# Reading three of four batches in large loads: a gated linear attention and a feed-forward layer on one core

## The chip, the cores and the metric

The kernel runs on one core of a Trainium2 chip. The metric is the device time of one execution in microseconds. Two runs of the kernel before took 193.17 and 194.55 us, median 193.86. A profiled execution gives the trace that this document reads; its span, from the first to the last instruction of the program, is 192.0 us.

The core has a matrix engine (PE, with its weight loads shown apart as PEld), a vector engine (DVE), an activation engine (ACT), GpSimd (POOL), and a sync engine (SP), which issues every DMA transfer of this kernel on one queue. The queue is served by 16 DMA engines.

## What is computed

Gated linear attention over 4 batches, 8 heads, 768 steps and 48 dimensions, followed by a feed-forward layer over the 3072 tokens:

```python
for t in range(S):
    state = alpha[:, :, t, :, None] * state + np.einsum('bhd,bhe->bhde', k[:, :, t], v[:, :, t])
    y[:, :, t] = np.einsum('bhd,bhde->bhe', q[:, :, t], state)
...
x = y.transpose(0, 2, 1, 3).reshape(B * S, H * D)      # 3072 x 384
h = x @ w_in                                           # 384 -> 2048
r = np.maximum(h, 0.0)
out = (s * (r * r) + b) @ w_out                        # 2048 -> 384
```

Inputs and outputs are 32-bit floats. q, k, v and alpha have 4.72 MB each.

## The kernel before

The sequence is cut into 24 blocks of 128 steps, six to a batch. A block n goes through these steps, named by the functions that issue them:

- Four loads (`load`, L192 to L197), one for each of alpha, q, k, v: 128 partitions (the steps) by 8 heads by 48 floats, 196,608 bytes, in pieces of 192 bytes, since consecutive steps of a head go to different partitions. Each tensor has five buffers (`NIN`), so the load of block n + 5 may be issued when block n has been read.
- `st_ln` (ACT) takes the logarithm of alpha; `st_cum` (PE) sums it along the steps; `st_exp_b` and `st_exp_i` (ACT) give the gates b and 1/b; `st_qb` and `st_kb` (DVE) multiply q and k by them; `st_vcast` (POOL) casts v.
- q and k are transposed: blocks 0 to 7 (`NPE`) by PE into PSUM with a copy on DVE (`st_T`, `st_Tcopy`), later ones by a DMA transpose on the SP queue (`st_Tdma`, L355).
- `st_A` (PE) makes the products of q and k, `st_mask` (DVE) masks them, `st_KV` (PE), `st_t1` (DVE) and `st_snew` (POOL) carry the state on, `st_y` (PE) makes the block's output and `st_yevac` (ACT) moves it to SBUF as the input of the feed-forward layer. From block 9 (`NAY`) y(n-1) is issued together with A(n).
- The feed-forward layer works on groups of one or two blocks (`GROUPS`): `mm1` units (PE) into two PSUM banks, `relu` (ACT), `square` (DVE) into a ring of 12 blocks (`RING`, `gt_sb`), then four `mm2` quads (PE) to a block into two banks `o_ps`, `oevac` (DVE) into three buffers `o_sb`, and `ostore`, a store on the SP queue.

The weights come in eight loads of 768 KB through four staging buffers `wst`, are cast by ACT and, for w_out, summed by DVE (`colsum_part`, `colsum_add`).

The order of the instructions on each engine is written out ahead by a planner, `Schedule` (L43 to L130): every step is an `op` with an engine, a planned duration, a priority, what it reads and what it writes. The planner plays these through with its own durations (a block load 1.02 us on SP, a DMA transpose 1.95) and emits the instructions in the order that comes out. On the chip each engine then runs its list strictly in this order, and waits at each instruction for the semaphores that it needs. So a wait on PE or on SP holds everything behind it. The DMAs take turns on eight semaphores; each waits for the landing of the one eight before it.

`LOADS` (L41) gives the order of the first loads, between which the weights stand.

The functions that the change touches, and what calls them:

Of the kernel before, what the change touches and what calls it, by code (L numbers as in the profile page):

```python
# [18 lines left out]
UNIT = 0.756  # L19
LEAD = {1: 98.3, 2: 224.9, 4: 115.8}  # L20

NPE = 8

NAY = 9

RING = 12

NST = 4

TB = 1.02  # L30
TW = 2.15
FILL_GAP = 0.45

P_BM, P_CS, P_BMM = -5, -380.7, 485.1
P = dict(
# [98 lines left out]
def kernel(  # L134
# [20 lines left out]
    d_model = moe_w_in.shape[0]  # L155
    d_ff = moe_w_in.shape[1]
    NJ = d_ff // 128
    NIN = 5

    sb = ctx.enter_context(tc.tile_pool(name="sb", bufs=1))  # L160
    ps = ctx.enter_context(tc.tile_pool(name="ps", bufs=1, space=bass.MemoryType.PSUM))
# [13 lines left out]
    def many(name, n, shape, dtype, zero=None):  # L175
        tiles = []
        for i in range(n):
            t = sb.tile(shape, dtype, name=f"{name}{i}")
            if zero is not None:
                zero.memset(t, 0.0)  # L180
            tiles.append(t)
        return tiles


    a_in = many("a_in", NIN, [128, H, D], FP32)
    q_in = many("q_in", NIN, [128, H, D], FP32)
    k_in = many("k_in", NIN, [128, H, D], FP32)
    v_in = many("v_in", NIN, [128, H, D], FP32)
    s_col = sb.tile([128, 1], FP32, name="s_col")
    b_col = sb.tile([128, 1], FP32, name="b_col")  # L190

    def load(n, src, dst):  # L192
        b, c = n // NCH, n % NCH
        nc.sync.dma_start(  # L194
            out=dst[n % NIN],
            in_=src[b, :, c * C : (c + 1) * C, :].rearrange("h s d -> s h d"),
        )  # L197

    for src, dst in ((alpha, a_in), (q, q_in), (k, k_in), (v, v_in)):
# [28 lines left out]
    w_in_bf = sb.tile([128, 3, d_ff], BF16, name="w_in_bf")  # L228
    w_out_bf = sb.tile([128, NJ, d_model], BF16, name="w_out_bf")
    QW = 4 * d_model  # L230
    wst = many("wst", NST, [128, QW], FP32)
    colsum = sb.tile([128, 2 * d_model], FP32, name="colsum")
    colpart = sb.tile([128, 2 * d_model], FP32, name="colpart")
    bones = sb.tile([128, 128], FP32, name="bones")
# [63 lines left out]

    def st_ln(n):
        nc.scalar.activation(  # L300
            out=la_sb[n % 2][:, :, 0:D], in_=a_in[n % NIN], func=AF.Ln
        )

    def st_cum(n):
# [21 lines left out]
    def st_vcast(n):  # L326
        nc.gpsimd.tensor_copy(  # L327
            out=vp_sb[n % 4].rearrange("a p (x d) -> a p x d", d=D)[:, :, 0:3:2, :],
            in_=v_in[n % NIN].rearrange("a (p e) d -> a p e d", e=2),
        )  # L330

    def st_qb(n):
        nc.vector.tensor_tensor(  # L333
            out=qk_sb[n % 3][:, 0, :, 0:D], in0=q_in[n % NIN], in1=b_sb[n % 2], op=ALU.mult
        )

    def st_kb(n):
        nc.vector.tensor_tensor(  # L338
            out=qk_sb[n % 3][:, 1, :, 0:D],
            in0=k_in[n % NIN],  # L340
            in1=binv_sb[n % 2],
            op=ALU.mult,
        )
# [213 lines left out]
    op("ACT", 2.2, -9000, lambda: None)  # L557
    SRC = {"a": (alpha, a_in), "q": (q, q_in), "k": (k, k_in), "v": (v, v_in)}
    loads = list(LOADS)
    for n in range(1, NBLK):  # L560
        loads += [f"{x}{n}" for x in "aqkv" if f"{x}{n}" not in LOADS]

    def load_op(x, n):
        op("SP", TB, loads.index(f"{x}{n}") - 1000, load, n, *SRC[x], w=[(x, n % NIN)], lat=2.0)

    stage = 0
    for x in range(4):
        op("SP", 1.4 if x == 0 else 0.85, -2000 + x, lambda: None, w=[("aqkv"[x], 0)], lat=2.0)
    for rank, item in enumerate(loads):
        t, i = rank - 1000, int(item[1:])  # L570
        if item[0] in "aqkv":
            if i < NIN:
                load_op(item[0], i)
# [28 lines left out]
    def add_block(n):  # L602
        i2, i3, ii = n % 2, n % 3, n % NIN
        t = want(n)
        if n >= NIN:
            for x in "aqkv":
                load_op(x, n)
        op("ACT", 0.45, t + P["ln"], st_ln, n, r=[("a", ii)], w=[("la", i2)])
        op("PE", 0.27, t + P["cum"], st_cum, n, r=[("la", i2)], w=["ct"], lat=0.16)
        op("ACT", 0.41, t + P["eb"], st_exp_b, n, r=["ct"], w=[("b", i2)])  # L610
        op("ACT", 0.49, t + P["ei"], st_exp_i, n, r=["ct"], w=[("bi", i2), ("bl", i2)])
        op("POOL", 0.5, t + P["vc"], st_vcast, n, r=[("v", ii)], w=[("vp", n % 4)], lock=True)
        op("DVE", 0.48, t + P["qb"], st_qb, n, r=[("q", ii), ("b", i2)], w=[("qb", i3)], lock=True)
        op("DVE", 0.48, t + P["kb"], st_kb, n, r=[("k", ii), ("bi", i2)], w=[("kb", i3)], lock=True)
# [12 lines left out]
        late = n + 1 < NBLK and n + 1 >= NAY  # L627
        if n >= NAY:
            r1, w1 = ys.pop(n - 1)
            op("PE", 0.935, want(n - 1) + P["Ay"], st_Ay, n, r=rA + r1, w=wA + w1, lat=0.16)  # L630
            yevac_op(n - 1)
        else:
            op("PE", 0.43, t + P["A"], st_A, n, r=rA, w=wA, lat=0.16)
        op("DVE", 1.14, t + P["mk"], st_mask, n, r=["a"], w=[("am", i2)])
        rr = [("am", i2), ("qkT", i3), ("vp", n % 4)] + ([] if first(n) else [("S", (n - 1) % 3)])
        if late:
            ys[n] = (rr, ["py"])
        else:
            op("PE", 0.6, t + P["y"], st_y, n, r=rr, w=["py"], lat=0.16)
            yevac_op(n)  # L640
# [29 lines left out]
                op("SP", 0.55, -2000, ostore, x, r=[("os", (x // 4) % 3)])  # L670

    for n in range(NBLK):
        add_block(n)

        if n and n >= NAY and blk_group[n - 1][0] != blk_group[n][0]:
            add_group(blk_group[n - 1][0])
        if (n + 1 < NAY or n + 1 == NBLK) and n + 1 == first_blk[blk_group[n][0]] + GROUPS[blk_group[n][0]]:
            add_group(blk_group[n][0])

    def fill(idle, at):
        for _ in range(int((idle - FILL_GAP) / (0.22 if at < 9.0 else 0.12))):
# [35 lines left out]
```

## Time and profile before

| what | value |
|---|---|
| median of two runs | 193.86 us |
| span of the profiled execution | 192.0 us (1.8 less than the median) |
| PE busy | 175.3 us, 91% |
| DVE, ACT, POOL busy | 135.9, 109.5, 33.3 us |
| DMA queue of SP | 124,192 packets, 34.09 MB, 82.6% of 16 engines' span |
| read from and written to HBM | 25.17 MB, 4.72 MB |
| last matmul ends | 188.5 us |
| mean granted clock of PE | 0.991 |

How to read the profile: the page gives each engine's busy time and, in 40 equal slices of 4.8 us, the busy share in tenths. The DMA line is the mean busy share of the 16 DMA engines. The table by stretches gives the same for chosen stretches of the span. The chain of waits follows back from the last instruction what released what. In lists of instructions a line starts with the time since the span's start and the duration; "x6" are instructions run together. Matmuls are pipelined, and their ends are modelled, so the distance between starts tells more than a busy time.

### The profile page before, as it was taken

What the parts mean: (1) busy time and instruction counts of PE and PEld (TensorE: products, weight loads), DVE (VectorE), ACT (ScalarE), POOL (GpSimd) and SP (SyncE); (2) the same over time, 40 slices, a digit from 0 to 9 for tenths busy, and PEclk for the clock granted to TensorE, in tenths of its full rate; (3) what the DMA queues carried; (4) which work ended last, traced back from release to release, by engine and by line L of the source; (5) the groups of instructions that cost most, each with busy time, mean ns of one, the idle gap of its engine ahead of it and who ended that gap; (6) DMA issues with size and microseconds to landing.
All of it is one profiled execution on the core that took longest, in us unless ns stands there. A gap on an engine that the chain in (4) does not pass through costs nothing.

```text
span 192.0 us, 5369 instructions
## 1 busy us (share of the span) xinstructions
PE 175.3 (91%) x2153; PEld 126.7 (66%) x2153; DVE 135.9 (71%) x256; ACT 109.5 (57%) x225; POOL 33.3 (17%) x60
## 2 busy tenths in 40 slices
PE   1877688879999999999999999999999999999992
PEld 0555467657677767777777766776766876777761
DVE  4643299989799898877689868587777786554421
ACT  3254789984357847767475754763663763654300
POOL 8402022103120431201122313011131131000000
PEclk9996999999999999999999999999999999999999
DMA  6989979999999999999999998897998895011112
GB/s 122 203 219 317 312 161 245 353 223 205 196 232 193 219 140 213 197 214 188 196 160 209 145 236 188 171 207 169 208 197 195 164 180 144 3 43 41 40 45 82
DMA packets 124218, 34.44 MB, mean 179 GB/s; under 512 B 117536, under 2 KB 122656, under 8 KB 124192
## 3 DMA queue, kind: packets, MB, share of 16 engines
q1 hardware_dynamic: 124192, 34.09, 82.6%
q8 instruction: 17, 0.28, 0.6%
q14 instruction: 9, 0.07, 0.1%
HBM read 25.17 MB, written 4.72 MB: 156 GB/s over the span
## 4 chain that ended last, share of the span: by engine, by line
PE 66%; DMA 14%; DVE 8%; SPq 7%; ACT 2%; issue 1%
PE o_ps L515 29%; PE h_ps L490 25%; PE py_ps L444 5%; DMA wst<-in_moe_w_in_dram 4%; DMA q_in<-in_q_dram 4%; SPq L194 4%; DMA wst<-in_moe_w_out_dram 3%; PE a_ps L406 3%; SPq L240 3%; DMA qkT<-qk 3%; DVE am L415 2%; PE py_ps L364 2%; PE ct_ps L306 1%; DVE gt L506 1%; ACT r L499 1%
## 5 line engine op out<-in xcount | busy, mean ns | idle before, releaser
L490 PE MATMUL h_ps<-xd,w_in_bf 128*128 128x256 bf16 (+1 forms) x624 | 74.8, 264 | 0.8 <-ACT r L499 0.5
L499 ACT ACTIVATE r<-h_ps 128x512 bf16<-128x512 f32 x96 | 56.5, 601 | 32.3 <-PE h_ps L490 22.8
L515 PE MATMUL o_ps<-w_out_bf,gt 128*128 128x384 bf16 x384 | 72.8, 326 | 2.0 <-ACT w_out_bf L261 2.0
L490 PEld LDWEIGHTS <-w_in_bf 128*128 128x128 bf16 x624 | 54.7, 98 | 10.8 <-issue 1.2
L506 DVE TENSOR_TENSOR gt<-r 128x512 bf16<-128x512 bf16 x96 | 43.5, 465 | 21.7 <-ACT r L499 21.1
L515 PEld LDWEIGHTS <-gt 128*128 128x128 bf16 x384 | 36.0, 98 | 21.2 <-issue 2.3
L415 DVE TENSOR_TENSOR am<-a_ps,mask 128x1024 bf16<-128x1024 f32 x24 | 29.3, 1220 | 1.6 <-PE a_ps L406 1.4
L327 POOL CAST vp<-v_in 128x384 bf16<-128x384 f32 x24 | 13.3, 553 | 95.0 <-DMA v_in<-in_v_dram 84.7
L526 DVE SCALAR_TENSOR_TENSOR o_sb<-o_ps,s_col,bias_w 128x384 f32<-128x384 f32 x24 | 14.8, 616 | 10.0 <-PE o_ps L515 9.6
L300 ACT ACTIVATE la<-a_in 128x384 bf16<-128x384 f32 x24 | 12.5, 521 | 14.1 <-DMA a_in<-in_alpha_dram 13.9
L400 POOL TENSOR_TENSOR s_st<-t,blast 128x384 bf16<-128x384 bf16 x16 | 14.5, 909 | 30.8 <-DVE t L389 23.0
L468 ACT ACTIVATE xd<-py_ps 128x384 bf16<-128x384 f32 x24 | 11.8, 491 | 13.0 <-PE py_ps L444 12.8
L338 DVE TENSOR_TENSOR qk<-k_in,binv 128x384 bf16<-128x384 f32 x24 | 13.4, 558 | 6.7 <-ACT binv L323 5.5
L333 DVE TENSOR_TENSOR qk<-q_in,b_s 128x384 bf16<-128x384 f32 x24 | 13.5, 564 | 5.2 <-ACT b_s L320 4.1
L320 ACT ACTIVATE b_s<-ct_ps 128x384 f32<-128x384 f32 x24 | 11.7, 488 | 6.8 <-PE ct_ps L311 6.7
L389 DVE TENSOR_TENSOR t<-py_ps,s_st 64x192 bf16<-64x192 f32 x32 | 11.3, 353 | 3.9 <-PE py_ps L364 3.2
L306 PE MATMUL ct_ps<-la,U_bf 128*128 128x384 bf16 x24 | 8.0, 334 | 6.3 <-ACT la L300 6.3
L323 ACT ACTIVATE binv<-ct_ps 128x384 f32<-128x384 f32 x24 | 11.8, 490 | 0.0
L311 PEld LDWEIGHTS <-la 128*128 128x128 bf16 x96 | 6.0, 97 | 7.7 <-issue 5.6
L406 PE MATMUL a_ps<-qkT 64*128 64x128 bf16 x192 | 9.8, 222 | 1.0 <-DVE qkT L373 0.7
L406 PEld LDWEIGHTS <-qkT 64*128 64x128 bf16 x192 | 5.5, 96 | 7.3 <-issue 4.3
L444 PE MATMUL py_ps<-am,vp 128*32 128x128 bf16 x384 | 9.8, 224 | 0.5 <-DVE am L415 0.5
(42 smaller groups left out, 108.1 us busy)
## 6 DMA issues: line engine op xcount, KB each, us to landing
a_in<-in_alpha_dram SPq DMA_DIRECT2D x24, 192.0 KB, 3.9
q_in<-in_q_dram SPq DMA_DIRECT2D x24, 192.0 KB, 3.9
k_in<-in_k_dram SPq DMA_DIRECT2D x24, 192.0 KB, 3.9
v_in<-in_v_dram SPq DMA_DIRECT2D x24, 192.0 KB, 3.7
out_dram<-o_sb SPq DMA_DIRECT2D x24, 192.0 KB, 2.6
wst<-in_moe_w_in_dram SPq DMA_DIRECT2D x4, 768.0 KB, 8.4
wst<-in_moe_w_out_dram SPq DMA_DIRECT2D x4, 768.0 KB, 7.0
qkT<-qk SPq DMA_TRANSPOSE x16, 3.7
```

Source lines behind the costliest of these rows:

```text
L327: nc.gpsimd.tensor_copy(out=vp_sb[n % 4].rearrange("a p (x d) -> a p x d", d=D)[:, :, 0:3:2, :], in_=v_in[n % NIN].rearrange("a (p e) d -> ...
L333: nc.vector.tensor_tensor(out=qk_sb[n % 3][:, 0, :, 0:D], in0=q_in[n % NIN], in1=b_sb[n % 2], op=ALU.mult)
L338: nc.vector.tensor_tensor(out=qk_sb[n % 3][:, 1, :, 0:D], in0=k_in[n % NIN], in1=binv_sb[n % 2], op=ALU.mult,)
L400: nc.gpsimd.tensor_tensor(out=s_sb[n % 3], in0=t1_sb[n % 2], in1=bl, op=ALU.mult)
L406: nc.tensor.matmul(out=a_ps[:, e, p, :], lhsT=qkT[64 * e : 64 * e + 64, 1, p, :], rhs=qkT[64 * e : 64 * e + 64, 0, p, :], start=True, stop ...
L415: nc.vector.tensor_tensor(out=am_sb[n % 2].rearrange("a e p t -> a (e p) t"), in0=a_ps.rearrange("a e p t -> a (e p) t"), in1=mask.unsquee ...
L444: nc.tensor.matmul(out=y_ps[32 * (x % 4) : 32 * (x % 4) + 32, x // 4, :], lhsT=(st[:, p, c0 : c0 + 32] if e is None else vp[:, p, c0 + 48 ...
L490: nc.tensor.matmul(out=hp[:, i * n : (i + 1) * n], lhsT=w_in_bf[:, kk, 128 * j : 128 * (j + 1)], rhs=xd_sb[g % 3][:, kk, 0:n], start=(kk = ...
L499: nc.scalar.activation(out=r_sb[w % 2], in_=h_ps[w % 2], func=AF.Relu)
L506: nc.vector.tensor_tensor(out=gt_sb[:, js[0] : js[0] + len(js), c0 : c0 + n], in0=r, in1=r, op=ALU.mult)
L515: nc.tensor.matmul(out=op[:, 0:d_model], lhsT=gt_sb[:, j, c0 : c0 + C], rhs=w_out_bf[:, j, :], start=(j == 0), stop=(j == NJ - 1),)
L526: nc.vector.scalar_tensor_tensor(out=ots, in0=o_ps[(x // 4) % 2][:, 0:d_model], scalar=s_col, in1=bias_w, op0=ALU.mult, op1=ALU.add,)
```

## The change

The four inputs move into two sets of buffers, each of which holds a whole batch of all four tensors. The blocks of batch 0 are loaded one by one as before. Batches 1, 2 and 3 are loaded tensor by tensor: one load of 1,179,648 bytes brings a tensor's six blocks (`load_batch`). The loads of batch 1 stand behind the 24 block loads; those of batch 2 are ordered behind the k products of blocks 8 to 11, those of batch 3 behind those of blocks 14 to 17 (`BATCH_AT`; this is an order in the planner's list, not a wait on the chip). The four staging buffers of the weights become a part of the second set, so batch 1's alpha, q and k wait for the casts and sums that read them. PE transposes blocks 0 to 6 instead of 0 to 7, and the ring has 10 blocks instead of 12. At the end five more loads of q (`probe`) are issued into the first set, in pieces of 2, 3, 4 and 6 rows and of one row; what they bring is not used. They overlap in the buffer, so each waits for the one before.

```diff
-NPE = 8
+NPE = 7
-RING = 12
+RING = 10
+TBATCH = 3.2
+BATCH_AT = {1: 1, 2: 8, 3: 14}
...
-    a_in = many("a_in", NIN, [128, H, D], FP32)
-    q_in = many("q_in", NIN, [128, H, D], FP32)
-    k_in = many("k_in", NIN, [128, H, D], FP32)
-    v_in = many("v_in", NIN, [128, H, D], FP32)
+    in_sb = many("in_set", 2, [128, 4, H, NCH, D], FP32)
+    a_in, q_in, k_in, v_in = range(4)
+
+    def block_in(x, n):
+        return in_sb[n // NCH % 2][:, x, :, n % NCH, :]
...
+    def load_batch(b, src, dst):
+        nc.sync.dma_start(
+            out=in_sb[b % 2][:, dst].rearrange("a h c d -> a (h c) d"),
+            in_=src[b].rearrange("h (c p) d -> p (h c) d", p=C),
+        )
...
-    wst = many("wst", NST, [128, QW], FP32)
+    stage_sb = in_sb[1].rearrange("a x h c d -> a (x h c d)")
+    wst = [stage_sb[:, QW * i : QW * (i + 1)] for i in range(NST)]
...
-    for n in range(1, NBLK):
+    for n in range(1, NCH):
         loads += [f"{x}{n}" for x in "aqkv" if f"{x}{n}" not in LOADS]
+
+    NIN = 2 * NCH
...
+    def batch_op(x, b):
+        held = [("wst", i) for i in range(NST)] if b == 1 else []
+        op("SP", TBATCH, 4 * b + "aqkv".index(x) - 900, load_batch, b, *SRC[x],
+           r=[("begun", n) for n in [BATCH_AT[b] + "aqkv".index(x)] if b > 1],
+           w=[(x, (NCH * b + c) % NIN) for c in range(NCH)] + held, lat=2.0)
+
+    flat = in_sb[0].rearrange("a x h c d -> a (x h c d)")
+
+    def probe(m):
+        if m:
+            nc.sync.dma_start(
+                out=flat[:, 0 : H * m * D].rearrange("a (h r) -> a h r", h=H),
+                in_=q[0, :, 0 : m * C, :].rearrange("h (p r) d -> p h (r d)", p=C),
+            )
+        else:
+            nc.sync.dma_start(
+                out=flat[:, 0 : 64 * H * NCH].rearrange("a (j d) -> a j d", d=64)[:, :, 0:D],
+                in_=q[0].rearrange("h (c p) d -> p (h c) d", p=C),
+            )
...
-        if n >= NIN:
-            for x in "aqkv":
-                load_op(x, n)
...
     for n in range(NBLK):
+        for b in BATCH_AT:
+            if 0 <= n - 1 - BATCH_AT[b] < 4:
+                batch_op("aqkv"[n - 1 - BATCH_AT[b]], b)
         add_block(n)
...
+    for m in (2, 3, 4, 6, 0):
+        op("SP", 2.0, 5000, probe, m, r=[("qkT", (NBLK - 1) % 3)], w=["probe"])
```

More of the change, by code (lines that the diff above doesn't have):

```diff
@@ L157 @@
     NJ = d_ff // 128
-    NIN = 5
     sb = ctx.enter_context(tc.tile_pool(name="sb", bufs=1))
@@ L194, in load @@
         nc.sync.dma_start(
-            out=dst[n % NIN],
+            out=block_in(dst, n),
             in_=src[b, :, c * C : (c + 1) * C, :].rearrange("h s d -> s h d"),
+        )
[3 more added lines that the diff above has]
+            in_=src[b].rearrange("h (c p) d -> p (h c) d", p=C),
         )
@@ L300, in st_ln @@
         nc.scalar.activation(
-            out=la_sb[n % 2][:, :, 0:D], in_=a_in[n % NIN], func=AF.Ln
+            out=la_sb[n % 2][:, :, 0:D], in_=block_in(a_in, n), func=AF.Ln
         )
@@ L328, in st_vcast @@
             out=vp_sb[n % 4].rearrange("a p (x d) -> a p x d", d=D)[:, :, 0:3:2, :],
-            in_=v_in[n % NIN].rearrange("a (p e) d -> a p e d", e=2),
+            in_=block_in(v_in, n).rearrange("a (p e) d -> a p e d", e=2),
         )
@@ L333, in st_qb @@
         nc.vector.tensor_tensor(
-            out=qk_sb[n % 3][:, 0, :, 0:D], in0=q_in[n % NIN], in1=b_sb[n % 2], op=ALU.mult
+            out=qk_sb[n % 3][:, 0, :, 0:D], in0=block_in(q_in, n), in1=b_sb[n % 2], op=ALU.mult
         )
@@ L339, in st_kb @@
             out=qk_sb[n % 3][:, 1, :, 0:D],
-            in0=k_in[n % NIN],
+            in0=block_in(k_in, n),
             in1=binv_sb[n % 2],
@@ L571 @@
         if item[0] in "aqkv":
-            if i < NIN:
-                load_op(item[0], i)
+            load_op(item[0], i)
             continue
@@ L613, in add_block @@
         op("DVE", 0.48, t + P["qb"], st_qb, n, r=[("q", ii), ("b", i2)], w=[("qb", i3)], lock=True)
-        op("DVE", 0.48, t + P["kb"], st_kb, n, r=[("k", ii), ("bi", i2)], w=[("kb", i3)], lock=True)
+        op("DVE", 0.48, t + P["kb"], st_kb, n, r=[("k", ii), ("bi", i2)], w=[("kb", i3), ("begun", n)], lock=True)
         if n < NPE:
```

## The prediction, made before the changed kernel ran

> **What bounds the kernel now.** I read the page first: busy shares and the 40 slices.
>
> ```profile
> PE 175.3 (91%) x2153; PEld 126.7 (66%) x2153; DVE 135.9 (71%) x256; ACT 109.5 (57%) x225; POOL 33.3 (17%) x60
> ...
> PE   1877688879999999999999999999999999999992
> ...
> DMA  6989979999999999999999998897998895011112
> ```
>
> PE has no gap after slice 10 (48 us), and the DMA engines hardly any from 20 us to 160: two resources are full at once, and the order in which the queue serves them decides. The table by stretches says the same in numbers:
>
> ```profile
> 20.00:48.00 28.00, 23.58 (x336) 18.17 (x336) 23.50 (x41) 23.15 (x41) 4.64 (x6) 1.00 0.98 248
> 48.00:66.00 18.00, 18.00 (x245) 12.52 (x243) 16.01 (x31) 11.15 (x28) 2.99 (x7) 1.00 1.00 209
> 66.00:100.00 34.00, 34.00 (x434) 25.14 (x431) 27.54 (x55) 21.56 (x48) 6.95 (x10) 1.00 0.99 190
> ```
>
> (Stretch, its length, busy us of PE, PEld, DVE, ACT and POOL, granted clock, DMA share, GB/s.) Up to 48 us PE starves on first loads and weights; then it is never idle.
>
> What a load costs the DMA engines shows in the DMA view of 44 to 48 us, where nothing but block loads moves:
>
> ```profile
> DMA packets 4219, 0.80 MB, mean 200 GB/s; under 512 B 4219, under 2 KB 4219, under 8 KB 4219
> ...
> q1 hardware_dynamic: 4219, 0.80, 102.6%
> ```
>
> 0.80 MB in 4219 packets is 190 B each, one 48-float row; 16 engines x 4 us x 1.026 / 4219 = 15.6 ns per piece per engine. Several loads were queued, so this is no latency but the engines' rate for such pieces. The same view of 33.6 to 38.4 us, where half of the packets are weight rows of 1.5 KB, has
>
> ```profile
> DMA packets 2046, 1.69 MB, mean 353 GB/s; under 512 B 1072, under 2 KB 2046, under 8 KB 2046
> ```
>
> so the rate goes with the size of the piece.
>
> That one queue serves in order shows at the transposes (L355). Issue to landing is min/median/max
>
> ```profile
> DMA to landing us min/median/max: 3.0/3.7/4.9
> ```
>
> and the 4.9 is the piece of the chain of waits at 106 us, where two loads had been issued just ahead (104.15 and 104.59):
>
> ```profile
> 105.88 0.55 DVE qk L338
> 106.43 0.03 DVE gt L506
> 106.46 4.92 DMA qkT<-qk
> 111.38 0.05 issue
> 111.42 0.40 PE a_ps L406 x8
> ```
>
> PE takes up A(15) 0.04 us after the landing: there is little room behind a transpose.
>
> **The change, part by part.** Times are those of the profiled execution: span 192.0, 1.8 below the median of the runs (193.86); I add that 1.8 to every span.
>
> *Up to A(5), nothing.* The first 34 DMAs stand in the same order and carry the same bytes in the same 192 B pieces. Their SBUF side becomes strided for blocks 0 to 5; bounds nothing to one more packet cost per piece; I take nothing, since the pieces were counted as 192 B when the SBUF side was one 1,536 B run. A(5) stands at 51.7 us in the PE timeline. What PE has left from there I count in the changed program's order, by starts in the timeline: 80 mm1 units x 0.655, 87 mm2 quads x 0.65, 19 y (16 x 0.51, 3 x 0.34), 19 A x 0.33, 18 cum x 0.27, 18 KV x 0.17, one T 0.45: 132.5 us. Before it is 133.0 (T(7) more), and that took 136.8, to 188.5. So if no wait is added the time is 193.86 - 0.45 = **193.4**. There is nothing else to win: the change takes no other work off PE.
>
> *Batch loads.* 72 block loads become 12 of 6144 pieces. At 200 GB/s one takes **5.9 us**. Lower bound 3.4 (the weights' 353 GB/s), upper 6.2 (190 GB/s, 66 to 100 us). I take 5.9: the pieces stay 192 B, and 200 GB/s is the row of such pieces alone. The planner laid out the new order with 3.2 (TBATCH), so that order has no room for the difference. SP issues 54 rows fewer; it was not the bound, so this is worth nothing, and if issuing one batch takes SP some us, the queue is busy with that batch meanwhile.
>
> The Trainium skill, "DMA: Bandwidth & Descriptors", section "Rules for kernel authors", says the opposite: use 1 MiB or more per DMA, and merge small transfers into one; its table of measurements gives 341 GB/s at 1 MB. By that page a batch would take an estimated 3.5 us. No run here shows that size with such pieces; the rate is rival 1.
>
> *Batch 1 (blocks 6 to 11).* Before, cum(6) needed one load of 0.98 us; now it needs a whole batch. v5 is issued at 43.51 and lands 4.2 later, 47.7. The first batch (alpha) lands 5.9 later, 53.6; Ln 0.52; cum(6) at 54.2 instead of 52.0: stall 2.2. Batch q lands at 60.1 (a store of 0.6 between). Batch k stands on SP behind the stores of blocks 1 and 2, of which the second waits for o_sb at about 57.7; q still fills the queue then, so k lands at 60.1 + 1.2 + 5.9 = 67.2, v at 73.1. PE reaches T(6) at 54.2 + 10.5 of work = 64.7; kb(6) is done at 67.8: stall 3.1. Then A(6), cum(7), cum(8), KV(6) at 73.9 (v and 0.55 of cast); after two more quads all matmul work of blocks 0 to 5 is used up. y(6), its evacuation, KV(7), A(7), mask 1.22, y(7), the transpose of block 8 behind the last evacuation on DVE: A(8) at about 79.5. Without stalls PE would be there at 51.7 + 19.5 = 71.2. Lost: **8.3**. (The casts and column sums of the staging area end at 42.5 and 42.3, before the batch loads over it are issued at 44.7 to 58: that wait is nothing.)
>
> *Batch 2 between the transposes.* On SP: T8, a, T9, q, T10, k, T11, v, T12. Each T waits for a whole batch in the queue ahead of it. T itself takes 1.2 to 1.75 of the queue (it lands 0.8 to 2.7 after the load ahead of it); I take 1.5. So A(8) to A(12) takes 4 x (5.9 + 1.5) = 29.6, against 18.4 of PE work standing there: 11.2 lost, and 1.2 more since KV(12) needs v of the same batch. Lost: **12.4**, A(12) at 110.3.
>
> *Batch 3.* a stands before T14, q before T16, k before T17, v between T18 and T19. The same sum against PE's work: 0.6 at A(14), 1.8 at A(16), 1.9 at A(17), 2.7 at KV(18). Lost: **7.0**.
>
> *NPE 7.* T(7) leaves PE (0.45, counted) and DVE (copy 0.69, not the bound), and adds 1.5 to the queue, inside batch 1's loss. *RING 10:* mm1 is at most some four blocks ahead of mm2 in the order; nothing.
>
> *Probes.* 4.13 MB, each waiting on SP for the landing of the one before: 12 to 21 us of data and five latencies of 2 (the fastest load lands 2.9 after its issue, 1 of it data): 22 to 31. Behind them on SP stand the stores of blocks 14 and 15, behind these DVE's evacuations (three o_sb), then PE (two o_ps). They begin after the store of block 13, with some 50 us of PE work to come, and the DMA engines are near idle there (slices 34 on): nothing, and 1 for 1 past that cover.
>
> Sum: 193.4 + 8.3 + 12.4 + 7.0 = **221**.
>
> A bound that needs no stall table: from 46.3 (v5's data in) the queue must carry 12 x 5.9 + 17 x 1.5 + 13 stores x 0.6 = 104 before T(23) lands at 151.7, and in the new order 42.4 us of PE work (24.8 before) follow A(23). With 1.2 of PE slack, 3.5 from last matmul to end and the 1.8: 201.
>
> **Clock.** Idle PE can cost more than the idle time:
>
> ```profile
> 12.30:15.70 3.40, 1.46 (x21) 1.08 (x22) 1.92 (x2) 1.48 (x1) 0.51 (x1) 1.00 0.65 176
> 15.70:19.10 3.40, 3.38 (x43) 2.27 (x40) 0.71 (x2) 1.49 (x1) 0.83 (x1) 0.52 1.01 320
> ```
>
> After 3.4 us with PE 43% busy, the next 3.4 ran at 0.52. In the stretch A(8) to A(12) PE is busy about 60%, so single windows can fall that low; each costs at most 1.7, part of it inside a wait. I put nothing in the sum and up to 7 in the range. The Trainium skill, "TensorE: Matmul & The Clock Gate", section "Why this matters for your kernels", warns of idle gaps over about 3 us; the trace agrees, and lost the clock even with shorter gaps (longest 1.5). By that page only the 3 us waits count, two or three of them, an estimated 3 to 5 us.
>
> **Rivals.**
> 1. *A batch moves at the weights' rate* (353 GB/s, 3.4 us). Batch 1 then still empties PE around A(7) (mask, transpose latency): 2.9; A(8) to A(12) needs 4 x 4.9 = 19.6 against 18.4, unevenly (A(10) has 3.2 of PE work against 4.9): 3 in all. 193.4 + 6 = **200**. For: one long contiguous run per partition in SBUF. Against: the packets above. This is also where the page's rule leads.
> 2. *Not slower.* The engines pay per SBUF run (9,216 B a partition in a batch) and not per DRAM row. From 4 x (t + 1.5) = 18.4 a batch of t = 3.1 us or less (380 GB/s) hides every transpose; what stays is the chain around A(7), 1.8: **195**. Against: block loads had 1,536 B runs there and were still paid as 192 B.
> 3. *The queue is as forecast, but the rest reacts worse:* the half clock, or probes that hold the last stores: **232** and more.
>
> **Chances.** Forecast 0.84, rival 1 0.08, rival 2 0.05, rival 3 0.03. The range goes from rival 1 to the forecast plus clock and rounding of a dozen stalls, 200 to 232. About 2% is what a measurement here tells from no change: faster 0.01, same 0.05, slower 0.94.
>
> **What would show it.** Right: batch loads landing 6 us apart; transposes L355 with a median near 8 us; PE idle before A (L406) and cum(6) between 52 and 145, 25 to 30 us in all; last 40 us PE full. Wrong: GB/s above 300 while batches move, transposes near 4 us, or PE idle mostly in the last 40 us (probes).

## The result and the profile after

| | before | after |
|---|---|---|
| median of two runs (us) | 193.86 (193.17 to 194.55) | 224.45 (223.84 to 225.06) |
| span of the profiled execution (us) | 192.0 | 222.4 |
| PE busy (us), mean granted clock | 175.3, 0.991 | 182.5, 0.962 |
| packets of SP's queue | 124,192 | 74,704 |

The changed kernel takes 1.161 times as long (95% interval 1.143 to 1.179). That is 3.5 us above the forecast of 221 and inside its range of 200 to 232. Some runs of the experiments below are over 1.5% slower than the fastest of the same kernel; medians and ratios leave them out, and only the traces of e2_split and e11_reverse are of such runs.

The page of the changed kernel: busy shares, then the lines of the 40 slices (5.56 us each) for PE, the granted clock and the DMA engines, and the packet count.

```profile
PE 182.5 (82%) x2145; PEld 129.8 (58%) x2145; DVE 135.3 (61%) x255; ACT 110.9 (50%) x225; POOL 34.2 (15%) x60
...
PE   2875797797968774983997938969999999999993
...
PEclk9999999999999978598899996999999999999999
DMA  6999899998798486989979899783346573951011
...
DMA packets 74728, 38.81 MB, mean 174 GB/s; under 512 B 45008, under 2 KB 73168, under 8 KB 74704
```

Before, PE had no gap from slice 10 on. Now it has gaps up to slice 27 (150 us), which is where batch 3 has landed, and is full behind that. The DMA engines, hardly ever idle before, have dips between 60 and 150 us. The table by stretches (stretch, its length, busy us of PE, PEld, DVE, ACT, POOL, granted clock, DMA share, GB/s) gives this time first for the kernel before, then for the changed one:

```profile
60.00:150.00 90.00, 89.26 (x1129) 64.80 (x1127) 70.83 (x137) 54.36 (x123) 16.68 (x24) 1.00 1.00 191
60.00:150.00 90.00, 68.63 (x832) 47.08 (x831) 55.84 (x105) 43.74 (x101) 14.67 (x22) 0.91 0.92 186
```

So the queue is a little worse used: 0.92 instead of 1.00 of the time, 186 GB/s instead of 191. But the inputs as a whole do not come later. The last load of all, v of batch 3, lands at 149.4 us; before, v of block 23 landed at 159.2. What comes later is what is needed first: v of block 18, the first of batch 3, landed at 126.9 before and lands at 149.4 now.

The same table gives the stages of batches 2 and 3 and the rest:

```profile
80.00:113.00 33.00, 25.44 (x270) 17.08 (x266) 18.46 (x36) 15.43 (x36) 4.58 (x7) 0.79 0.96 188
113.00:152.00 39.00, 31.24 (x434) 22.41 (x434) 26.04 (x50) 20.14 (x47) 7.12 (x10) 0.96 0.93 185
152.00:182.00 30.00, 30.00 (x437) 21.89 (x435) 23.61 (x44) 16.66 (x36) 6.14 (x7) 1.00 0.51 124
```

In 80 to 113 us PE issued 270 matmuls; the kernel before issued 416 there, and its clock stayed at 1.00.

SP's own list from the first load of batch 2 on (start, and the time that SP spent on the issue):

```profile
78.21 0.71 SPq L203 DMA_DIRECT2D in_set<-in_alpha_dram  x1
79.53 6.64 SPq L365 DMA_TRANSPOSE qkT<-qk  x1
86.63 0.69 SPq L203 DMA_DIRECT2D in_set<-in_q_dram  x1
88.92 4.55 SPq L365 DMA_TRANSPOSE qkT<-qk  x1
93.94 0.69 SPq L203 DMA_DIRECT2D in_set<-in_k_dram  x1
```

A transpose is issued 0.9 to 2.3 us after a batch, and SP is held in that issue for 4.6 to 7.0 us (before, the issue took 1.2 to 2.2). The packet records show what ends it: the first one is let go at 86.2, as the transpose's own packets of 256 B begin at 86.0, where those of the batch end. Only then can SP issue the next batch, whose data start at 88.0, after a pause. The fine stretches show the pause: the DMA share falls from 0.97 to 0.68 between two batches. They show the clock too, 0.57 and 0.51 around the wait.

```profile
80.00:84.00 4.00, 4.00 (x30) 2.84 (x25) 3.14 (x6) 1.59 (x3) 1.10 (x2) 0.57 0.97 230
84.00:87.00 3.00, 0.87 (x11) 0.71 (x9) 0.89 (x3) 0.13 (x1) 0.82 (x1) 1.00 0.68 137
87.00:94.00 7.00, 6.08 (x62) 4.05 (x62) 2.34 (x3) 3.65 (x10) 0.00 (x0) 0.51 0.92 196
```

For all 17 DMA transposes together, issue to landing is min/median/max

```profile
DMA to landing us min/median/max: 3.0/4.8/8.8
```

The eight behind a batch take 6.4 to 8.8 each (seven of them 8.3 or more), the others 3.1 to 4.8.

What PE waited for, from its list of waits over the whole span (us in total, times, longest; "PE L316 <- ACT la" reads: PE at L316 waited for la on ACT):

```profile
PE ct_ps L316 <- ACT la L310: 7.7, 4, 4.3
...
PE h_ps L500 <- ACT r L509: 4.6, 4, 3.1
...
PE py_ps L374 <- POOL vp L337: 3.5, 3, 2.2
PE o_ps L525 <- DVE gt L516: 3.5, 1, 3.5
PE a_ps L416 <- DVE t L399: 3.5, 1, 3.5
PE ct_ps L360 <- DVE qk L348: 2.7, 1, 2.7
```

The 7.7 of L316 are mostly the start of the kernel; of them only 1.1 us, at cum(6), fall behind 48 us. The longest waits end at a DMA, though none names one. The 2.7 of L360 is T(6), which needs batch 1's k. The 3.5 of L416 is A(16) at 133.09; the transpose of block 16 landed at 133.05, and DVE's t had long been done. The 3.1 of L500 is a feed-forward unit at 87.9. It needs a PSUM bank that a relu empties, and that relu stands on ACT behind Ln(12), which waited for batch 2's alpha (landed 86.78). The 3.5 of L525 at 104.5 needs a square that stands on DVE behind kb(12), which waited for batch 2's k (landed 103.05).

In all, PE stood still for 22.6 us after 48 us (sum of the gaps over 0.06 us in its timeline), before for 0.7.

How fast a batch moves shows the DMA view of 46 to 52 us, with the first two batches and little else (106 packets of a store, 77 of the last block load):

```profile
DMA packets 1732, 1.36 MB, mean 227 GB/s; under 512 B 106, under 2 KB 1731, under 8 KB 1731
...
q1 hardware_dynamic: 1731, 1.34, 95.0%
```

1.36 MB in 1732 packets is 0.78 KB each: a batch goes out in packets of 768 bytes, four rows, and not in rows of 192. The rate is 227 GB/s, against 200 for the rows of the kernel before.

### The profile page after: what moved, and what is told of

The parts are those of the page before. It is cut to its first block, busy times and chain, and to the rows that moved or that the text cites. A ratio compares the mean times of both kernels' runs of the same rounds, so it can differ in the third digit from the quotient of the medians.

```text
span 222.4 us, 5253 instructions
## 1 busy us (share of the span) xinstructions
PE 182.5 (82%) x2145; PEld 129.8 (58%) x2145; DVE 135.3 (61%) x255; ACT 110.9 (50%) x225; POOL 34.2 (15%) x60
## 2 busy tenths in 40 slices
DMA packets 74728, 38.81 MB, mean 174 GB/s; under 512 B 45008, under 2 KB 73168, under 8 KB 74704
## 3 DMA queue, kind: packets, MB, share of 16 engines
q1 hardware_dynamic: 74704, 38.48, 75.7%
## 4 chain that ended last, share of the span: by engine, by line
PE 41%; DMA 33%; SPq 15%; DVE 5%; issue 2%; ACT 1%; POOL 1%; DVEq 0%; POOLq 0%; ACTq 0%
PE o_ps L525 18%; PE h_ps L500 16%; DMA in_set<-in_alpha_dram 11%; DMA in_set<-in_v_dram 10%; DMA in_set<-in_q_dram 8%; SPq L197 7%; DMA in_set<-in_k_dram 4%; PE py_ps L454 3%; SPq L250 2%; SPq L365 2%; PE a_ps L416 2%; DVE t L399 1%; SPq L203 1%; DVE am L425 1%; PE py_ps L374 1%
## 5 line engine op out<-in xcount | busy, mean ns | idle before, releaser
L500 PE MATMUL h_ps<-xd,w_in_bf 128*128 128x256 bf16 (+1 forms) x624 | 79.1, 274 | 4.7 <-ACT r L509 4.6
L525 PE MATMUL o_ps<-w_out_bf,gt 128*128 128x384 bf16 x384 | 75.7, 331 | 5.7 <-DVE gt L516 3.5
L500 PEld LDWEIGHTS <-w_in_bf 128*128 128x128 bf16 x624 | 57.6, 101 | 18.9 <-issue 5.8
L516 DVE TENSOR_TENSOR gt<-r 128x512 bf16<-128x512 bf16 x96 | 42.0, 447 | 28.1 <-ACT r L509 27.5
L525 PEld LDWEIGHTS <-gt 128*128 128x128 bf16 x384 | 36.1, 98 | 24.3 <-DVE gt L516 4.4
L337 POOL CAST vp<-in_set 128x384 bf16<-128x384 f32 x24 | 12.7, 546 | 88.9 <-DMA in_set<-in_v_dram 66.4
L410 POOL TENSOR_TENSOR s_st<-t,blast 128x384 bf16<-128x384 bf16 x16 | 16.0, 1002 | 49.9 <-DVE t L399 41.0
L348 DVE TENSOR_TENSOR qk<-in_set,binv 128x384 bf16<-128x384 f32 x24 | 13.5, 568 | 16.1 <-DMA in_set<-in_k_dram 8.6
L343 DVE TENSOR_TENSOR qk<-in_set,b_s 128x384 bf16<-128x384 f32 x24 | 14.5, 610 | 12.8 <-DMA in_set<-in_q_dram 7.7
L310 ACT ACTIVATE la<-in_set 128x384 bf16<-128x384 f32 x24 | 12.5, 526 | 15.1 <-DMA in_set<-in_alpha_dram 11.1
L330 ACT ACTIVATE b_s<-ct_ps 128x384 f32<-128x384 f32 x24 | 11.8, 493 | 10.4 <-PE ct_ps L321 10.3
L316 PE MATMUL ct_ps<-la,U_bf 128*128 128x384 bf16 x24 | 8.4, 351 | 8.2 <-ACT la L310 7.7
L416 PE MATMUL a_ps<-qkT 64*128 64x128 bf16 x192 | 10.2, 230 | 5.9 <-DVE t L399 3.5
L416 PEld LDWEIGHTS <-qkT 64*128 64x128 bf16 x192 | 5.8, 98 | 12.3 <-DMA qkT<-qk 6.7
L374 PE MATMUL py_ps<-vp,qk 128*128 128x96 bf16 x96 | 8.5, 215 | 4.3 <-POOL vp L337 3.5
## 6 DMA issues: line engine op xcount, KB each, us to landing
out_dram<-o_sb SPq DMA_DIRECT2D x24, 192.0 KB, 2.3
in_set<-in_alpha_dram SPq DMA_DIRECT2D x6, 192.0 KB, 5.0
in_set<-in_q_dram SPq DMA_DIRECT2D x6, 192.0 KB, 4.5
in_set<-in_k_dram SPq DMA_DIRECT2D x6, 192.0 KB, 4.1
in_set<-in_v_dram SPq DMA_DIRECT2D x6, 192.0 KB, 5.0
```

Of the source, the lines that this page charges most:

```text
L343: nc.vector.tensor_tensor(out=qk_sb[n % 3][:, 0, :, 0:D], in0=block_in(q_in, n), in1=b_sb[n % 2], op=ALU.mult)
L410: nc.gpsimd.tensor_tensor(out=s_sb[n % 3], in0=t1_sb[n % 2], in1=bl, op=ALU.mult)
L416: nc.tensor.matmul(out=a_ps[:, e, p, :], lhsT=qkT[64 * e : 64 * e + 64, 1, p, :], rhs=qkT[64 * e : 64 * e + 64, 0, p, :], start=True, stop ...
L500: nc.tensor.matmul(out=hp[:, i * n : (i + 1) * n], lhsT=w_in_bf[:, kk, 128 * j : 128 * (j + 1)], rhs=xd_sb[g % 3][:, kk, 0:n], start=(kk = ...
L516: nc.vector.tensor_tensor(out=gt_sb[:, js[0] : js[0] + len(js), c0 : c0 + n], in0=r, in1=r, op=ALU.mult)
L525: nc.tensor.matmul(out=op[:, 0:d_model], lhsT=gt_sb[:, j, c0 : c0 + C], rhs=w_out_bf[:, j, :], start=(j == 0), stop=(j == NJ - 1),)
```

## The experiments

Each ratio below is to runs of the kernel before on the same chip (their medians lie between 191.90 and 193.86 us). Differences in us in the text are worked out from these ratios, times 193.86. The ratio of the changed kernel rests on two runs, and its interval is 3.5 us to either side. A(n) is the start of the scores of block n on PE.

| kernel | median us | ratio (95%) | A(5) | A(8) | A(12) | A(18) | PE gaps after 48 |
|---|---|---|---|---|---|---|---|
| before | 193.86 | 1 | 51.7 | 70.0 | 90.8 | 132.7 | 0.7 |
| after | 224.45 | 1.161 (1.143 to 1.179) | 51.5 | 79.7 | 112.9 | 151.6 | 22.6 |
| e12_blocks | 197.50 | 1.030 (1.023 to 1.037) | 50.6 | 68.5 | 94.5 | 134.2 | 1.0 |
| e1_no_probes | 222.47 | 1.160 (1.150 to 1.169) | 49.9 | 76.4 | 109.4 | 148.0 | 23.0 |
| e2_split | 213.27 | 1.104 (1.094 to 1.115) | 51.5 | 76.7 | 107.0 | 142.5 | 15.7 |
| e11_reverse | 222.31 | 1.149 (1.141 to 1.157) | 52.9 | 81.9 | 114.5 | 153.1 | 23.2 |
| e10_half | 219.19 | 1.134 (1.127 to 1.141) | 51.8 | 78.1 | 110.2 | 146.1 | 20.3 |
| e4_pe_transpose | 211.11 | 1.093 (1.085 to 1.100) | 50.7 | 77.3 | 103.2 | 142.8 | 10.4 |
| e13_split_pe | 204.05 | 1.063 (1.057 to 1.069) | 51.9 | 74.2 | 100.1 | 136.9 | 3.3 |
| e5_act_queue | 224.86 | 1.167 (1.159 to 1.175) | 51.3 | 85.7 | 113.8 | 152.6 | 23.5 |
| e3_plan | 218.21 | 1.133 (1.125 to 1.141) | 50.6 | 84.2 | 114.2 | 155.5 | 18.6 |
| e14_early | 226.06 | 1.177 (1.170 to 1.183) | 51.2 | 87.3 | 111.8 | 149.2 | 25.3 |
| e7_warm | 223.52 | 1.167 (1.159 to 1.174) | 51.3 | 79.8 | 111.5 | 151.2 | 15.6 |
| e6_batch1_blocks | 252.87 | 1.308 (1.300 to 1.316) | 51.2 | 86.8 | 139.7 | 177.8 | 47.4 |

### Is it the batch loads at all?

All of the change but the batch loads:

```diff
-    for n in range(1, NCH):
+    for n in range(1, NBLK):
         loads += [f"{x}{n}" for x in "aqkv" if f"{x}{n}" not in LOADS]
...
-        op("SP", TB, ..., load, n, *SRC[x], w=[(x, n % NIN)], lat=2.0)
+        op("SP", TB, ..., load, n, *SRC[x],
+           r=["wfree", ("begun", n - 5)] if n >= NCH else [], w=[(x, n % NIN)], lat=2.0)
...
+    op("SP", 0.0, -1000, lambda: None, w=[("wst", i) for i in range(NST)] + ["wfree"], lat=0.0)
...
-        for b in BATCH_AT:
-            if 0 <= n - 1 - BATCH_AT[b] < 4:
-                batch_op("aqkv"[n - 1 - BATCH_AT[b]], b)
+        if n >= NCH:
+            for x in "aqkv":
+                load_op(x, n)
```

> Everything of the change is kept (two batch sets, weights staged in the second set, seven transposes on the tensor engine, ring of 10, probe loads), only batches 1 to 3 are read block by block as before, each block's loads waiting until the block five earlier has used its k. Theory (the batch loads alone cost the 30 us): 192 to 197 us. Rival (the shared staging space, the transpose moved to the queue or the smaller ring cost something of their own): 200 us or more, and block 8's scores later than 72 us.

It took 197.50 us, half a us above the theory's 192 to 197 and below the rival's 200; A(8) starts at 68.5, before the 72 that the rival names. PE has no gap to speak of (1.0 us) and its last matmul ends at 187.25 us; in the trace of the kernel before that is 188.5, on a chip where it takes 2.0 us longer. So sharing the staging space, the moved transpose and the smaller ring cost PE next to nothing. By the ratios the batch loads cost 25 of the 31 us. What is left in this kernel is mostly its tail: from the last matmul to the end it needs 7.7 us, the kernel before and the changed kernel 3.6. As the changed kernel has no such tail, the batch loads make nearly all of its loss. SP's list at the end (L594 is the last probe, L548 the output stores):

```profile
176.40 0.53 SPq L548 DMA_DIRECT2D out_dram<-o_sb  x1
181.76 0.83 SPq L594 DMA_DIRECT2D in_set<-in_q_dram  x1
182.68 9.94 SPq L548 DMA_DIRECT2D out_dram<-o_sb  x4
```

The chain of waits ends with the store of 182.68, which lands behind that probe:

```profile
182.68 8.84 DMA out_dram<-o_sb
```

The last evacuation into `o_sb` needs the buffer of that store and starts at 191.64, 4.4 us after the last matmul. In the changed kernel the same probes are over 20 us before the end. That the probes make this tail is read from the chain; no run had the block loads without the probes.

The probes alone, taken away (their data are used by nothing, so the output is the same):

```diff
-    for m in (2, 3, 4, 6, 0):
-        op("SP", 2.0, 5000, probe, m, r=[("qkT", (NBLK - 1) % 3)], w=["probe"])
```

> The changed kernel without the five probe loads at the end (their data is used by nothing). My theory: the probes lie under the last 50 us of PE work, so the time stays that of the changed kernel, 224.5 us, within 1. Rival (probes hold the last stores, these the evacuations, these PE): 2 to 6 us shorter, 218 to 222.

222.47 us, a ratio of 1.160 against 1.161 with them, on a chip that runs the kernel before in 192.18: in the changed kernel they cost nothing that can be measured, though the intervals leave room for 4 us either way. Together the two runs suggest that the same five loads are free while PE has 50 us of work left as the first is issued (167.5 of 218.8), and no longer are with 24 us left (163.5 of 187.3).

### Whole-batch landing

Each batch load as six block loads at the same place, block 6 (12, 18) first, and then in reverse:

```diff
-        nc.sync.dma_start(
-            out=in_sb[b % 2][:, dst].rearrange("a h c d -> a (h c) d"),
-            in_=src[b].rearrange("h (c p) d -> p (h c) d", p=C),
-        )
+        for c in range(NCH):              # e11: reversed(range(NCH))
+            load(NCH * b + c, src, dst)
```

> Each batch load is replaced, at its place in the order, by the six block loads of 192 KB that bring the same bytes; nothing else is changed. My theory: what costs is the place of these bytes ahead of the transposes in the queue and their rate per 192-byte row, not the size of a transfer; six loads take 6 x 0.98 = 5.9 us where the trace of the changed kernel shows 5.3 to 5.9 for a batch, so 224.5 to 229 us. Rival A (one very long transfer is itself the harm, shorter ones let a transpose through earlier): below 216. Rival B (large transfers are much faster than small ones, so that splitting them costs a lot): 235 or more.

> As e2_split, but the six block loads of each batch are issued last block first, so that block 6, 12 or 18, which is needed first, lands last, as it does in a batch load, where everything lands at once. Theory G (e2_split gained because a batch load tells of its landing only when all six blocks are in, some 5 us after the first block is): most of the gain goes, 219 to 223 us, with KV(6) back near 73 us and KV(18) near 148. Theory S (it gained because one long transfer holds SP and lets the queue run dry between batches and transposes): 211 to 215, as e2_split.

The first took 213.27 us, 11 less than the changed kernel, where I had expected no gain; it lies where rival A has it. I had counted the bytes and their place in the queue, and not what the large load costs: the first block of a batch lands only when the sixth has. The reversed order, with the same loads and the same bytes, takes 222.31, where theory G has it. That is 2 us below the changed kernel, inside the interval: with the first block landing last, the short transfers win next to nothing. The casts of v in POOL's list, those that waited for a load of v, show when v of a batch's first block is there (the last column is the idle time before, and what ended it). With the blocks in order, 67.57 (block 6) and 138.78 (block 18):

```profile
67.57 0.51 POOL L335 CAST vp<-in_set 128x384 bf16<-128x384 f32 x1 [19.23 <-DMA in_set<-in_v_dram]
...
138.78 1.68 POOL L335 CAST vp<-in_set 128x384 bf16<-128x384 f32 x3 [9.33 <-DMA in_set<-in_v_dram]
```

In reverse, the casts of a batch come all at once (x4, x3), when the last block load has landed:

```profile
73.68 1.87 POOL L335 CAST vp<-in_set 128x384 bf16<-128x384 f32 x4 [23.92 <-DMA in_set<-in_v_dram]
...
111.72 1.41 POOL L335 CAST vp<-in_set 128x384 bf16<-128x384 f32 x3 [16.81 <-DMA in_set<-in_v_dram]
...
150.22 1.41 POOL L335 CAST vp<-in_set 128x384 bf16<-128x384 f32 x3 [15.21 <-DMA in_set<-in_v_dram]
```

And the changed kernel, the same picture as the reverse:

```profile
72.85 1.86 POOL L337 CAST vp<-in_set 128x384 bf16<-128x384 f32 x4 [24.49 <-DMA in_set<-in_v_dram]
...
149.51 1.40 POOL L337 CAST vp<-in_set 128x384 bf16<-128x384 f32 x3 [14.92 <-DMA in_set<-in_v_dram]
```

So some 9 us (1.104 against 1.149) hang on which block lands first, at equal bytes and equal transfers.

### The transposes behind the batches

All transposes on PE, none on the queue:

```diff
-NPE = 7
+NPE = 24
```

> The changed kernel with all 24 transposes on PE; no DMA transpose is left in the queue, the batch loads stand next to each other there. PE gets 17 transposes x 0.45 = 7.7 us more, DVE 17 copies x 0.69 = 11.7. My theory (from A(8) on the loss is transposes behind batch loads in the queue): the stalls before A(9) to A(17) go, what stays is batch 1 (about 9) and some wait for v of batch 2; 193 + 8 + 9 = 207 to 214 us. Rival (the loss is the late data of the batches themselves): 222 or more.

211.11 us, as expected, and 13 less than the changed kernel, though PE now has 17 x 0.45 = 7.7 us more to do. Batch 2 lands at 82.4, 88.4, 94.6 and 99.9, on average 5.8 apart, and the stretch of batch 2 is nearly full, at full clock (columns as above):

```profile
80.00:113.00 33.00, 31.22 (x429) 23.81 (x429) 27.96 (x54) 19.99 (x46) 5.93 (x9) 1.00 0.59 135
```

What is left of the gaps (10.4 us) lies in batch 1, 7.1 us before 84, and at KV(18), 2.6 us, which waits for v of batch 3. The run takes away the transposes' wait behind the batches and their own time in the queue (DMA share 0.59 here, 0.96 in the changed kernel); it does not tell the two apart.

Both together, block loads in order and all transposes on PE:

> Block loads in the batch order (first block of a tensor lands first) and all 24 transposes on the tensor engine, so that none stands in the queue behind a batch. If the two losses are separate (10 to 11 us by the one, 12 by the other, less what the tensor engine then has to do more): 202 to 207 us. If they are the same loss seen twice: 209 to 213 us, as the better of the two alone.

204.05 us, in the range for separate losses. 11 and 13 alone make 24; together they give 19, so they overlap by some 5 us. The bound for this kernel is 193.4 + 7.7 = 201.1, and by its ratio it takes 206.1. Of the 5 us between, the gaps that are left make 3.3, most of them at 72 to 81 us, in batch 1.

Each batch in two loads of four heads. A block needs both, so whole-batch landing stays; the single transfer is shorter:

```diff
+        for e in range(2):
+            hh = slice(H // 2 * e, H // 2 * (e + 1))
-            out=in_sb[b % 2][:, dst].rearrange("a h c d -> a (h c) d"),
-            in_=src[b].rearrange("h (c p) d -> p (h c) d", p=C),
+            out=in_sb[b % 2][:, dst, hh].rearrange("a h c d -> a (h c) d"),
+            in_=src[b, hh].rearrange("h (c p) d -> p (h c) d", p=C),
```

> Each batch load is cut into two loads of four heads each, 0.59 MB, all six blocks in both. Every block still lands only with the second half. Theory G (landing of the whole batch at once is the harm): no change, 221 to 226 us. Theory S (the length of one transfer is the harm): about half of e2_split's gain or more, 214 to 219.

219.19 us, 5 less, between the two ranges and next to that of theory S. The halves go out in 192-byte rows again (the page has 118,928 packets under 512 B, against 45,008), and the transposes' issue holds SP for at most 4.8 us instead of 7.0. From the landing of block 8's transpose to that of block 12's it is 30.3 us instead of 32.9. The lines of that kernel's transposes (min/median/max of the issue in ns, first and last start) and their landing:

```profile
L367 SPq DMA_TRANSPOSE qkT<-qk x17: 1231/1359/4762, 70.9 to 159.8; - x17
...
DMA to landing us min/median/max: 3.0/4.8/6.8
```

So about 5 us may go with the length of one transfer, though its bytes are the same. That isn't settled: in e11_reverse the transfers are shorter still, the first block also lands last, and only 2 us are won.

The batches on a queue of their own, issued by ACT:

```diff
-        nc.sync.dma_start(
+        nc.scalar.dma_start(
             out=in_sb[b % 2][:, dst].rearrange("a h c d -> a (h c) d"),
```

> The twelve batch loads are issued by ACT, on its own DMA queue, at the same places of the written-out order; transposes, block loads and stores stay on SP's. My theory (transposes are late because they stand behind a batch in one queue served in order): with two queues a transpose need not wait for the batch; it lands in 4 to 6 us instead of up to 8.8, most of the 19 us that I put down to batches 2 and 3 goes away, batch 1 gains a little too since its k and v no longer stand behind stores: 203 to 213 us. Rival (the DMA engines are simply full, whatever the queue): 221 to 226.

224.86 us: nothing is won. My idea that a transpose would overtake a batch on another queue fell. Issue to landing of this kernel's transposes is worse in the median, 7.3 us instead of 4.8:

```profile
DMA to landing us min/median/max: 3.1/7.3/10.0
```

The packet records show why: from 80 to 83 us the transposes' packets (256 B) and the batch's (768 B) go out mixed and in equal number, 720 of each. Block 8's transpose went from 75.6 to 85.7. The Trainium skill, "DMA: Bandwidth & Descriptors", section "Queues, rings and completion order", says that an engine serves its queues by turns, packet by packet. The equal numbers agree with it, though the records don't tell the engines apart. ACT's own list also lets some batches go later (q of batch 2 at 89.47 instead of 86.63), so the run doesn't price the sharing alone.

### Order and start

The planner told the true length of a batch, `TBATCH = 5.9` instead of 3.2:

> The planner is told 5.9 us for a batch load instead of 3.2; every load and every result stays, only the order in which the engines take up their work changes. My theory: part of the loss is that PE's list was laid out for loads that come too early; with the longer duration the list has 87 us of PE work behind A(12) instead of 95 and 37 behind A(23) instead of 42, so 213 to 219 us. Rival (the loss is the queue alone, the order on PE doesn't matter): 223 to 226.

218.21 us, in the range. The blocks come later (A(8) at 84.2, A(18) at 155.5), but feed-forward work stands where the waits are, and from A(23) to the end 41 us are left instead of 46. 5 us of the loss are thus the order's: work that was ready stood behind work that waited.

Batches 2 and 3 three blocks earlier:

```diff
-BATCH_AT = {1: 1, 2: 8, 3: 14}
+BATCH_AT = {1: 1, 2: 5, 3: 11}
```

> Batches 2 and 3 issued three blocks earlier (after blocks 5 and 11 instead of 8 and 14). If the loss is that the read-ahead starts too late, batch 2 follows batch 1 in the queue, is there by 105 instead of 110 us, and the time is 214 to 219 us. If the queue's work is the bound until block 18, or the transposes behind the batches are, then nothing is won: 222 to 227 us, since the same bytes and the same transposes stand in one line.

226.06 us: nothing is won. Batch 2's alpha now goes ahead of batch 1's q, so batch 1's v lands at 78.5 instead of 72.7 and A(8) starts at 87.3; A(12) and A(18) are 1 and 2.5 us earlier than in the changed kernel, and the end later. An earlier start doesn't help, because what is issued earlier stands ahead of what is needed sooner.

### The clock

110 spare matmuls where PE stood still, for example

```diff
     def st_Ay(n):
+        warm({14: 10, 16: 26}.get(n, 0))
```

> Changed kernel plus 110 spare matmuls (128x256, 0.12 us each at full clock, into the scores' PSUM tile while nothing needs it) put where the tensor engine stood still for 1.5 to 3.5 us: before block 7's output, a matmul unit at 88, one at 104.5, the scores of blocks 14 and 16 and the state product of block 18. They keep the engine busy, and change nothing else. If the half clock after these waits is what the end is late by over my sum (3.4 us): the granted clock goes from 0.962 to 0.98 or more and the time to 219 to 222 us. If all of the lost clock reached the end (five windows of 3.4 us, half of each): 216 us. If the next wait for the loads swallows it: 223 to 226 us, at a higher clock.

The clock rose from 0.962 to 0.985 and the time stayed: 223.52 us, a ratio of 1.167 against 1.161. (The spare matmuls count as busy, so part of the smaller gaps in the table is they.) The table of this kernel for the stretches that had run at half speed:

```profile
80.00:84.00 4.00, 3.97 (x47) 3.35 (x42) 3.44 (x6) 1.68 (x4) 1.20 (x2) 1.00 0.99 212
84.00:87.00 3.00, 2.31 (x22) 1.93 (x20) 1.04 (x4) 1.49 (x5) 0.82 (x1) 1.00 0.58 111
87.00:94.00 7.00, 6.80 (x94) 5.27 (x91) 3.54 (x6) 3.69 (x10) 1.10 (x1) 1.00 1.11 184
```

PE is 1.4 us earlier at A(12), 2.5 us at A(16) (130.56 against 133.09), and then waits: v of batch 3 lands at 148.9 as it did (149.4), and from A(18) to the end both kernels take 70.8 us. One group of 26 stood one quad too early, so the gap of 3.5 us that it was to fill is still there at 103.3; it can hide a gain by A(12), not the wait for v behind it. The rival holds: the next wait for the loads swallows what the clock gives.

### A variant that measured something else

Batch 1 as 24 block loads, batches 2 and 3 as they are:

```diff
-                batch_op("aqkv"[n - 1 - BATCH_AT[b]], b)
+                if b > 1:
+                    batch_op("aqkv"[n - 1 - BATCH_AT[b]], b)
+        if n == 2:
+            for m in range(NCH, 2 * NCH):
+                for x in "aqkv":
+                    op("SP", TB, 4 * m + "aqkv".index(x) - 900, load, m, *SRC[x],
+                       w=[(x, m % NIN)] + [("wst", i) for i in range(NST)], lat=2.0)
```

> Batch 1 is read block by block, 24 loads of 192 KB in the order in which the blocks are needed; batches 2 and 3 stay batch loads. My theory: A(6) to A(8) return to their places before the change (57 to 72 us), a gain of some 8 us at A(8); but the queue must still carry 24 block loads and four batch loads before A(12), 46 + 23.5 + 22 + 9 + 5 = 106 us against 112.9, so only 6 to 8 of it reach A(12), and the order has 87 us of PE work behind A(12) instead of 95: 208 to 216 us. Rival (batch 1 costs little, the transposes behind batches 2 and 3 everything): 220 or more.

252.87 us, a miss. In the plan each of these loads writes the staging buffers, so the planner set each behind the landing of the one before, some 3 us apart, and placed the later ones behind stores and transposes that wait for earlier blocks. SP's list shows it:

```profile
64.15 0.36 SPq L548 DMA_DIRECT2D out_dram<-o_sb  x1
64.55 0.43 SPq L197 DMA_DIRECT2D in_set<-in_v_dram  x1
...
81.11 1.24 SPq L365 DMA_TRANSPOSE qkT<-qk  x1
```

The v load at 64.55 stands behind a store that waits until 64.15, and from 73.3 on nothing is issued until 81.1: a load waits for a block, and the block for a load. This is the order of this variant, and says nothing on batch 1 alone. e12_blocks, with one release of the staging space for all loads, is what it should have been.

## Why the prediction was right, point by point

- **Floor 193.4, PE's work unchanged.** e12_blocks bears it out: without batch loads the last matmul ends at 187.25 (A(5) was 1.1 earlier than before). The list of PE's remaining work adds up to 132.8 us, not 132.5; only the 0.45 of T(7) enters the sum. The tail that the probes add there is the text's "1 for 1 past that cover".
- **Batch load 5.9 us.** The reason was wrong and the size right, which is in part luck. The pieces don't stay rows of 192 B at 15.6 ns; they become packets of 768 B at 56 ns on average (median 46), which is 14 ns a row. 227 GB/s makes a batch 5.2 us of data, and without transposes batches land 5.8 apart (e4_pe_transpose). The sign that the text gave, landings 6 us apart, is seen only there: in the changed kernel they are 5.9 to 11.0 apart within a batch, since stores and transposes stand between.
- **Batch 1, 8.3 lost.** A(8) at 79.7, forecast 79.5. The four landings were 52.5, 59.4, 66.8 and 72.7 (53.6, 60.1, 67.2 and 73.1).
- **Batch 2, 12.4 lost.** A(12) at 112.9, forecast 110.3. This is the term that was too small. The transposes of blocks 8 to 12 landed at 79.6, 88.0, 95.3, 104.0 and 112.5, so 8.4, 7.3, 8.7 and 8.5 apart where the sum had 7.4. In "T itself takes 1.2 to 1.75 of the queue" I left out that SP is held in the issue until the batch ahead is through, so that the next batch begins late. The sum took it that "the queue is busy with that batch meanwhile"; here it had run dry. PE's gaps in this stretch are only 7.6 us. Most of the rest is matmuls at half clock (four windows of 3.4 us), which fill time that the landings set anyway.
- **Batch 3, 7.0 lost.** From A(12) to the end the sum has 219.2 - 110.3 = 108.9 us, measured were 109.5. Its parts fit less well than their sum: gaps of 1.5 at A(14), 3.5 at A(16), none at A(17) and 2.2 at KV(18), where the text had 0.6, 1.8, 1.9 and 2.7. The three differences (0.2, 2.4 and 0.6) are the 3.2 us by which the span missed.
- **Where PE waits.** 22.6 us of gaps instead of 25 to 30, and two of the three longest not before A or cum but before mm1 and mm2, by way of ACT and DVE, whose order puts a step that waits for a batch ahead of steps that don't. I had followed the queue and PE, and not these two. "Last 40 us PE full" holds, and "transposes L355 with a median near 8 us" holds for the eight behind a batch, not for all 17. The median of all is 4.8, nearer to the 4 that the text gave as a sign against it.
- **Clock: nothing in the sum.** Right by e7_warm, for a reason that the text had only in passing ("part of it inside a wait"). PE lost about 8.5 us of full-speed time in the whole span (222.4 us at 0.962), and hardly any of what e7_warm won back of it reached the end; two windows at half clock were left there. The estimate of 3 to 5 us by the Trainium skill's page "TensorE: Matmul & The Clock Gate", section "Why this matters for your kernels", isn't seen as time. That the clock falls after such gaps is seen: five windows of 3.4 us ran at half. But the one from 80.3 to 83.7 followed gaps of 1.5 us at most.
- **Probes, ring, NPE: nothing.** Right as far as e1_no_probes and e12_blocks can tell. The probes took 29.4 us (22 to 31 forecast) and began 51 us before the last matmul ended.
- **Rival 1, a batch at the weights' rate.** Fell: 216 to 227 GB/s (60 to 66 and 46 to 52 us). The Trainium skill, "DMA: Bandwidth & Descriptors", section "Rules for kernel authors", asks for 1 MiB or more per transfer, and the page's table of transfers issued from GpSimd has 341 GB/s at 1 MB. The same row has 6.15 us for that 1 MB, which would be an estimated 7 us for a batch; the prediction took the rate. Here 1.18 MB of 192-byte rows stay at two thirds of that rate, and e2_split, which goes back to 192 KB, is 11 us faster.
- **Rival 2, not slower.** Fell with it.

What stays open: how the 9 to 11 us of landing order, the 13 of the transposes, up to 5 of the transfer's length and the 5 of the order share out. They overlap, and only the first two were tried together.

## What to carry to other kernels

A larger transfer is worth what its rate gains, here 8 to 13%, and costs the wait of its first consumer for its last byte. Where the first part is needed at once, issue it first as a load of its own. On a queue that serves in order, ask of each long transfer what small, urgent one stands behind it; moving the long one to another queue did not help here, since the packets of both queues took turns. And don't count a lost clock or a filled gap as time until the next wait for the same bottleneck has been looked at.

## What the runs showed of the hardware

- A load of 48 rows of 192 B per partition goes out in packets of 768 B, one of 8 or 24 rows (block load, half batch) in packets of 192 B. No run here varied the number between 24 and 48.
- Larger packets alone bring little when the rows stay scattered: 192 B took 15.6 ns on average, the 768 B of a batch 56 (median 46). The 768 B of a probe whose pieces are contiguous on both sides took 46 (median 36), with little else in the queue.
- The issue of a DMA transpose holds SP while a batch is ahead of it: 4.6 to 7.0 us instead of 1.2 to 2.2. A batch issued behind another batch holds it as well, 4.9 to 5.9 us in e4_pe_transpose.
